# Dividing batch 0's outer products by head pairs, with one copy into the matmul bank

## The chip, the cores and the metric

The kernel runs on one core of a Trainium2 chip. The metric is device time in microseconds of one execution. Three executions of the kernel before took 101.63, 102.16 and 102.23 us; the median is 102.16.

## What is computed

Polynomial linear attention is followed by a two-layer network without a gate. The shapes are 4 batches, 4 heads, 1088 positions, head size 32, sketch size 8; 4352 tokens of 128 numbers, a hidden layer of 2048.

```python
a = einsum('rd,bhsd->bhsr', S1, x); b = einsum('rd,bhsd->bhsr', S2, x)
phi(x) = outer product of a and b, 64 features per position
kv = einsum('bhsf,bhsd->bhfd', phi(k), v);  z = phi(k).sum(over positions)
attn = (phi(q) @ kv) / (phi(q) @ z + 1e-6)
x = attn as (4352, 128)
h = x @ w_in;  g = h - tanh(h);  out = g @ w_out
```

## The kernel before

Every operation is an object with a name, the engines that may run it, and the tiles it reads and writes (`P.add`). A table of tokens (`TABLE`, line 27) sets the order: each token is the number of an operation, the letter of its engine (v VectorE, a ScalarE, g GpSimd, t TensorE, s SyncE) and, after a colon, the buffer or PSUM bank that a tile takes from its list. Every engine runs its own tokens strictly in the order of the table, and waits on semaphores for what it depends on (`sync`, line 244). `F` and `f` are fill matmuls on zeros at the start. Operations marked `lock` on VectorE and GpSimd wait for the other engine's last locked operation ahead of them in the table.

The work on keys, per batch b: transposes `kT` (line 579), the two sketches of the keys by matmul (`ksk`, line 599), their transposes back (`kab`, line 610), the Gram matrix of the two sketches (`gram`, `gm`, `scmm`, line 616 on), which gives the denominator; the outer products `w` of the two sketches, 64 per position and head (`k_outer`, and `k_outer0` for batch 0), and their product with v (`kvmm`, line 688). For queries: a transpose `qT`, sketches, a division and the outer products `qp`, their transposes `qpT`, and the numerators `num` (line 886), whose copies `x` (line 890) are the network's input `xT`.

Batch 0's first 384 columns take a way of their own, so that the network can start early (`q_lead`, line 743): the expanded sketches by matmul (`qA`, `qB`), the copies `bq0` and `bq1` of the second one out of PSUM on ScalarE, the products `qp0.0` and `qp0.1`, the denominator (`qac`, `abt`, `m0.0`, `den0.0`, `rd0.0`, `rdT`), the numerators `num0.0a` and `num0.1a`, and the tiles `x0.0a` and `x0.1a`. The remaining queries of batch 0 are transposed by `qT0.1` and run through `qsk0.3`, `abc0.3` and so on to `num0.3`.

Batch 0's keys: the tile `abk0` holds both sketches of all 9 blocks of 128 positions; its inner layout is (e, r, i), where head h = 2r + e, so `kab0.0` fills the head pair r = 0 and `kab0.1` the pair r = 1. `k_outer0` (line 670) cuts the nine blocks into four products, (0, 2), (2, 4), (4, 6) and (6, 9), all four heads in each. GpSimd makes the first two from SBUF (512 elements each), VectorE the other two (512 and 768 elements). For VectorE's two, ScalarE first copies the second sketch into a PSUM bank (`bps0`, `bps1`, line 678), and the product reads one operand from that bank (line 680). Each product has its own group of matmuls with v (`kvmm0.0` to `kvmm0.3`), which add up in the tile `pv[0]`. The result is copied and turned (`kvt0`, `kvt0t`, `kvc0`) for the numerators.

The network (`ffn`, line 972) takes ten groups of columns, 384, 352, 352, six times 512, and 192, with 16 blocks of the hidden layer each: `h` (line 984) into a PSUM bank, tanh `th` on ScalarE (line 988), from group 5 on for some columns the addition `dg` on VectorE (line 993), then `o` (line 1005), which adds up over the 16 blocks. The term without tanh goes through the combined weights `wch` and `wcl` (line 1009) where `dg` does not take it. The weights are cast to bf16 (`wi0` to `wi3`, `wo0` to `wo3`, line 934) and turned by the transposes `wit` (line 948) and their copies `wiT` (line 954). The output is transposed (`ot`, line 1014) and stored (`st`, line 1023).

PSUM has eight banks. Groups 0 to 6 use banks 0 to 2 for `h`, and bank 3 for the sum of `o`. The list `first1` (line 378), from which the small results of the head take a bank, leaves out bank 3.

Of the kernel before, what the change touches and what calls it, by code (L numbers as in the profile page):

```python
# [14 lines left out]
ALU = mybir.AluOpType  # L15
# [17 lines left out]
37s 237g 290t 31s 267t:2 268a:9 240a 269t:0 270a:10 132t:0 121v:1 41s 32s 273t:1 274a:11 279t:2 291t 35s 36s 292t 293t
280a:12 283t:0 284a:13 294t 271t:1 272a:14 122v:1 125v:1 275t:2 134v:0 43s 276a:15 89t:5 90a:0 133v 135t:3 136a:1
277t:0 278a:16 126v:0 123g:2 124v 44s 241g 246t:1 247t 137t 248a 57g 138v:0 139v 46s 285t:2 286a:17 295t 296t 55g
127t:0 53g 281t:0 129a 166v:1 165v 128v 297t 242g 298t 299t 13g 282a:18 48s 149v 316t:1 317a:19 322t:2 323a:0 318t:0
319a:1 167t:1 168v:1 324t:1 325a:2 54g 110s 328t:2 140g:4 300t 301t 169v 365t:0 366a:20 338t:1 184v 339a:21 141g:0
150t:0 320t:0 329a:22 383t:1 384a:23 109s 142g:3 40s 151v:1 249t:2 321a:28 250t 175g:1 251t 252t 9g 152v:0 153v:0 253v
369t:1 370a:29 393t:0 394a:3 170t:0 38s 143t:1 171a:0 144t 145t 310t:1 254v 326t:0 311a:4 327a:26 154v:0 302t 303t
146v:0 147s 314t:2 315a:27 172t 389t:1 173v:1 174v 304t 47s 390a:5 312t:0 313a:6 379t:2 380a:24 14g 185t:0 58g 305v:0  # L40
308s 342t:0 330t:1 371t:0 331a:25 177g:2 155g:0 158v:0 159v:1 372a:30 385t:2 386a:31 343t 344t 345t 346t 332t:1 333a:8
347t 348t 334t:0 349t 391t:2 350t 336t:1 351t 352t 186v:0 353t 335a:7 392a:9 337a:10 148s:1 340t:0 377t:2 156g:1 157v
354t 381t:1 115s 355t 356t 357t 358t 341a:32 359t 160g:2 378a:33 161v 114s 176v:4 387t:0 360v:1 382a:14 201v:1 373t:2
374a:11 367t:1 368a:34 162t:0 163v 187g:1 188v:1 388a:35 189v:1 164a 375t:2 376a:15 111s 395t:1 396a:16 397t:0 398t
399t 190g:1 193g:0 400t 401t 448t:0 449a:12 200v 436t:2 437a:18 112s 307s 446t:1 447a:13 45s 178t:2 179t 180t 219v
181v:1 194v:0 432t:0 433a:17 450t:2 451a:4 430t:1 431a:6 202t:0 182s 204v:0 203v 479t:0 480a:27 420t:2 195g:1 402t
403t 421a:19 434t:1 435a:1 183s:2 404t 405t 501t:0 502a:28 191g:2 211g:0 196v 205t:3 438t:2 439a:0 206v:1 210g:3 406t
407t 207t 422t:1 423a:2 116s 208v:0 209v 475t:0 476a:26 408t 489t:2 220t:0 192v 490a:22 428t:1 429a:25 424t:0 409t
410t 411t 412t 425a:8 413t 426t:2 497t:1 221v:1 306s 222v:0 487t:0 223v:0 224v:0 427a:7 488a:10 197t:0 481t:2 477t:0
414t 498a:21 199a 415v:2 482a:32 113s 440t:1 441a:20 213t:2 212g:1 214t 215t 198v 478a:34 216v:2 495t:2 225g:0 230g:0  # L50
309s 496a:29 545t:1 217s 231v:1 218s:3 608t:0 452t:0 453t 454t 455t 609a:30 610v 546a:11 620t:2 547v 228g:1 621a:15
622v 456t 457t 363s 505t:0 506a:33 458t 557t:1 459t 460t 361s 558a:24 559v 442t:2 229v 443a:14 461t 444t:0 445a:23
226g:2 462t 463t 503t:1 504a:31 554t:2 555a:35 227v 464t 465t 485t:0 486a:5 466t 493t:1 494a:9 556v 467t 468t 469t
470v:0 471s 483t:2 533t:0 534a:3 535v 572t:1 573a:16 574v 232t:0 234v 507t:0 484a:19 499t:0 500a:2 233v 542t:1 543a:8
# [251 lines left out]
def _vp(n):  # L306
    return {"vector": (n / 0.96 + 85.0, n / 0.96 + 215.0)}
# [6 lines left out]
def _a(n):  # L314
    return {"scalar": (n * 0.8333 + 62.0, n * 0.8333 + 203.0)}
# [6 lines left out]
def _gt(n):  # L322
    return {"gpsimd": (n * 1.76 + 120.0, n * 1.76 + 175.0)}
# [14 lines left out]
def bass_polysketch_attn__then__act_tanh_shrink_kernel(  # L338
# [316 lines left out]
    wvs = {}  # L655
# [8 lines left out]
            in1=abh(1)[:, :, None, :].to_broadcast([128, 12, 8, 8]),  # L664
            op=ALU.mult), r=[ab], w=[wv], name=f"w{b}.{p}", lock=True)

    bps = [_Val(first1) for _ in range(2)]
    K0 = [(0, 2), (2, 4), (4, 6), (6, 9)]

    def k_outer0():  # L670
        fs = lambda x, a, z: abk0[:, x, a:z].rearrange("p k (c i) -> p (k c) i", i=8)
        for p, (a, z) in enumerate(K0):
            wv = wvs[0, p] = _Val(w_p)
            nx = (z - a) * 4
            far = a >= 4
            if far:
                bp = bps[p - 2]
                P.add(_a(nx * 8), lambda e, n, a=a, z=z, bp=bp, nx=nx: e.copy(bp.ap[:, 0:nx * 8].rearrange("p (x i) -> p x i", i=8), fs(1, a, z)), r=ab0, w=[bp], name=f"bps{p - 2}")
            bsrc = lambda far=far, a=a, z=z, p=p, nx=nx: bps[p - 2].ap[:, 0:nx * 8].rearrange("p (x j) -> p x j", j=8) if far else fs(1, a, z)
            P.add(_vp(nx * 64) if far else _gt(nx * 64), lambda e, n, wv=wv, nx=nx, bsrc=bsrc, a=a, z=z: e.tensor_tensor(  # L680
                out=wv.ap[:, 0:nx * 64].rearrange("p (x i j) -> p x i j", i=8, j=8),
                in0=fs(0, a, z)[:, :, :, None].to_broadcast([128, nx, 8, 8]),
                in1=bsrc()[:, :, None, :].to_broadcast([128, nx, 8, 8]),
                op=ALU.mult), r=ab0 + ([bps[p - 2]] if far else []), w=[wv], name=f"w0.{p}", lock=not far)

    pv = [_Val(att1 if b else first1) for b in range(B)]

    def kv_mm(b):
        prev = None
        kc = K0 if b == 0 else [(0, 3), (3, 6), (6, 9)]  # L690

        def part(e, n, p):
            for blk in range(*kc[p]):
                for h in range(4):
                    x = (blk - kc[p][0]) * 4 + (h if b else h % 2 * 2 + h // 2)
                    i = e.matmul(pv[b].ap[h * 32:(h + 1) * 32, 0:64],  # L696
                                 vL[b][:, h, blk * 32:(blk + 1) * 32],
                                 wvs[b, p].ap[:, x * 64:(x + 1) * 64],
                                 start=(blk == 0), stop=(blk == 8), skip_group_check=True)
            return i  # L700
# [382 lines left out]
```

## Time and profile before

| what | value |
|---|---|
| median of 3 runs | 102.16 us |
| the profiled execution's own time | 101.74 us |
| its span, first to last instruction | 99.5 us |
| TensorE busy | 92.4 us |
| VectorE busy | 77.2 us |
| ScalarE busy | 78.4 us |
| GpSimd busy | 37.4 us |
| granted TensorE clock | 1.000 |

The profile records one execution. Each row of its timeline gives the start, the length, the engine (PE is TensorE, PEld its weight loads, DVE VectorE, ACT ScalarE, POOL GpSimd, SPq the DMA queue of SyncE), the line of the kernel, the operation, the tiles, shapes and the number of instructions, and in brackets how long the engine was idle before it and what ended that. Line 367 is a helper for copies, so rows with this line are told apart by their tiles. Lengths of records overlap a little within an engine. The tile names are those of memory: PSUM is always `psb`, batch 0's copies `bq` are written `th`, and the tanh tiles are written `th`, `wi_f` or `wo_f`, since they reuse this memory.

### The profile page before, as it was taken

What the parts mean: (1) busy time and instruction counts of PE and PEld (TensorE: products, weight loads), DVE (VectorE), ACT (ScalarE), POOL (GpSimd) and SP (SyncE); (2) the same over time, 40 slices, a digit from 0 to 9 for tenths busy, and PEclk for the clock granted to TensorE, in tenths of its full rate; (3) what the DMA queues carried; (4) which work ended last, traced back from release to release, by engine and by line L of the source; (5) the groups of instructions that cost most, each with busy time, mean ns of one, the idle gap of its engine ahead of it and who ended that gap; (6) DMA issues with size and microseconds to landing.
All of it is one profiled execution on the core that took longest, in us unless ns stands there. A gap on an engine that the chain in (4) does not pass through costs nothing.

```text
span 99.5 us, 3133 instructions
## 1 busy us (share of the span) xinstructions
PE 92.4 (93%) x1301; PEld 47.0 (47%) x1310; DVE 77.2 (78%) x144; ACT 78.4 (79%) x156; POOL 37.4 (38%) x57
## 2 busy tenths in 40 slices
PE   5987879999999999999999999999999999999980
PEld 2323543375366565635446444444444444444660
DVE  3097979999897999987857796757878899878630
ACT  4005149997886896989988998799999999998860
POOL 4046335288989473399979900000000000000000
PEclk9999999999999999999999999999999999999999
DMA  2996978799950468001700031510330553321627
GB/s 77 284 284 195 349 258 270 213 311 368 267 167 7 98 187 281 15 8 17 185 21 7 13 75 26 80 30 0 50 47 0 85 77 60 50 33 28 100 42 104
DMA packets 25541, 11.86 MB, mean 119 GB/s; under 512 B 19512, under 2 KB 23352, under 8 KB 25528
## 3 DMA queue, kind: packets, MB, share of 16 engines
q1 hardware_dynamic: 24440, 11.54, 44.5%
q10 hardware_dynamic: 1088, 0.13, 0.9%
q8 instruction: 10, 0.16, 0.7%
q14 instruction: 3, 0.02, 0.1%
HBM read 9.34 MB, written 2.33 MB: 117 GB/s over the span
## 4 chain that ended last, share of the span: by engine, by line
PE 79%; DVE 7%; ACT 4%; DMA 4%; issue 2%; POOL 0%; DVEq 0%
PE psb L984 31%; PE psb L1005 29%; PE psb L882 6%; DMA kL<-in_k_dram 4%; PE psb L599 3%; PE psb L1009 3%; PE psb L821 3%; ACT th L988 2%; DVE w L680 1%; PE psb L696 1%; DVE kT L579 1%; ACT wo_f L988 1%; DVE qp L768 1%; PE psb L962 1%; PE psb L761 1%
## 5 line engine op out<-in xcount | busy, mean ns | idle before, releaser
L988 ACT ACTIVATE th<-psb 128x512 bf16<-128x512 f32 (+3 forms) x83 | 45.1, 604 | 3.6 <-PE psb L984 2.8
L984 PE MATMUL psb<-xT,wi 128*128 128x512 bf16 (+3 forms) x154 | 42.5, 347 | 1.1 <-issue 0.3
L1005 PE MATMUL psb<-th,wo 128*128 128x512 bf16 (+3 forms) x94 | 25.9, 348 | 0.0
L984 PEld LDWEIGHTS psb<-xT,wi 128*128 128x128 bf16 x160 | 14.7, 98 | 19.3 <-ACT th L988 3.4
L993 DVE TENSOR_TENSOR th<-psb,th 128x320 bf16<-128x320 f32 (+2 forms) x28 | 14.9, 550 | 4.3 <-ACT th L988 4.0
L988 ACT ACTIVATE wi_f<-psb 128x512 bf16<-128x512 f32 (+3 forms) x28 | 16.7, 617 | 0.9 <-PE psb L984 0.8
L988 ACT ACTIVATE wo_f<-psb 128x512 bf16<-128x512 f32 (+3 forms) x25 | 14.2, 620 | 1.0 <-PE psb L984 0.6
L864 POOL TENSOR_TENSOR qp<-ap,abc 128x768 f32<-128x768 f32 x9 | 13.4, 1512 | 3.1 <-DVE qp L864 3.0
L1005 PEld LDWEIGHTS psb<-th,wo 128*128 128x128 bf16 x96 | 9.2, 98 | 8.2 <-DVE ot L1014 1.2
L661 POOL TENSOR_TENSOR w<-abk 128x768 f32<-128x768 f32 x8 | 11.9, 1512 | 0.9 <-DVE m L838 0.9
L869 DVE STREAM_TRANSPOSE qpT<-qp 128x768 f32<-128x768 f32 x11 | 10.5, 961 | 0.6 <-POOL qp L864 0.4
L1005 PE MATMUL psb<-wi_f,wo 128*128 128x512 bf16 (+2 forms) x34 | 10.2, 340 | 0.0
L1014 DVE STREAM_TRANSPOSE ot<-psb 128x512 f32<-128x512 f32 (+3 forms) x10 | 6.3, 631 | 4.0 <-PE psb L1005 4.0
L1005 PE MATMUL psb<-wo_f,wo 128*128 128x512 bf16 (+2 forms) x29 | 9.1, 352 | 0.1
L579 DVE STREAM_TRANSPOSE kT<-kL 128x512 f32<-128x512 f32 (+3 forms) x10 | 5.8, 602 | 2.8 <-DMA kL<-in_k_dram 2.8
L993 DVE TENSOR_TENSOR wi_f<-psb,wi_f 128x192 bf16<-128x192 f32 (+2 forms) x10 | 5.7, 565 | 1.6 <-ACT wi_f L988 1.4
L882 PE MATMUL psb<-qpT,kvb 32*32 32x288 f32 (+3 forms) x256 | 6.0, 379 | 0.0
L993 DVE TENSOR_TENSOR wo_f<-psb,wo_f 128x320 bf16<-128x320 f32 (+2 forms) x10 | 5.2, 547 | 0.8 <-ACT wo_f L988 0.5
L696 PE MATMUL psb<-w,vL 128*32 128x64 f32 x288 | 5.1, 221 | 0.6 <-issue 0.6
L442 PE MATMUL psb<-zz 128*128 128x512 bf16 x11 | 4.5, 596 | 1.1 <-DVE zz L440 1.1
L367 ACT COPY th<-psb 128x384 f32<-128x384 f32 x2 | 1.0, 480 | 5.6 <-PE psb L761 5.6
L826 DVE STREAM_TRANSPOSE abc<-psb 128x1152 f32<-128x1152 f32 (+1 forms) x4 | 5.0, 1262 | 0.3 <-PE psb L821 0.3
(100 smaller groups left out, 97.9 us busy)
## 6 DMA issues: line engine op xcount, KB each, us to landing
vL<-in_v_dram SPq DMA_DIRECT2D x16, 144.0 KB, 3.5
kL<-in_k_dram SPq DMA_DIRECT2D x6, 272.0 KB, 4.1
qL<-in_q_dram SPq DMA_DIRECT2D x6, 272.0 KB, 4.2
wi_f<-in_moe_w_in_dram SPq DMA_DIRECT2D x4, 256.0 KB, 4.7
wo_f<-in_moe_w_out_dram SPq DMA_DIRECT2D x4, 256.0 KB, 4.3
out_dram<-ot SPq DMA_DIRECT2D x15, 64.0 KB, 2.0
kL<-in_k_dram SPq DMA_DIRECT2D x1, 544.0 KB, 4.1
out_dram<-ot SPq DMA_DIRECT2D x8, 48.0 KB, 2.9
```

Of the source, the lines that this page charges most:

```text
L579: P.add(_v(nb * 32 * (r1 - r0)), lambda e, n, e_=e_, nb=nb, r0=r0, r1=r1: e.transpose(kTv[b][r0].ap.rearrange("p (j u t r) -> p r j u t", ...
L661: P.add({**_v(768), **_gt(768)}, lambda e, n: e.tensor_tensor(out=wv.ap.rearrange("p (x i j) -> p x i j", i=8, j=8), in0=abh(0)[:, :, :, N ...
L696: i = e.matmul(pv[b].ap[h * 32:(h + 1) * 32, 0:64], vL[b][:, h, blk * 32:(blk + 1) * 32], wvs[b, p].ap[:, x * 64:(x + 1) * 64], start=(blk ...
L826: P.add(_vp(sn * 4), lambda e, n: e.transpose(abc.ap.rearrange("p k h f -> p h k f")[:, :, 0:s1 - s0, :], psa4[:, :, 0:sn].rearrange("p h ...
L864: P.add({**_v(cn * 256), **_gt(cn * 256)}, lambda e, n, qp=qp, c0=c0, cn=cn: e.tensor_tensor(out=qp.ap[:, 0:cn * 256].rearrange("p (x i j) ...
L869: P.add(_v(cn * 256), lambda e, n, qp=qp, o0=o0, cn=cn: e.transpose(qt.ap[:, o0 * 256:(o0 + cn) * 256], qp.ap[:, 0:cn * 256]), r=[qp], w=[ ...
L882: i = e.matmul(psa4[h * 32:(h + 1) * 32, g, 0:kn * 32], (kvn[g * 32:(g + 1) * 32, h, x, :] if b else kvn[g * 32:(g + 1) * 32, h // 2, h % ...
L984: P.add(_mm(n_), lambda e, n, jb=jb, hv=hv: e.matmul(hv.ap[:, jb % m * 512:jb % m * 512 + n_], wi[jb // 4].ap[:, (jb % 4) * 128:(jb % 4 + ...
L988: act = P.add(_a(n_ * m), lambda e, n, hv=hv, th=th: e.activation(out=th.ap.rearrange("p (u x) -> p u x", u=m)[:, :, 0:n_], in_=hv.ap.rear ...
L993: P.add(_vp(gc * m), lambda e, n, hv=hv, th=th: e.tensor_tensor(out=th.ap.rearrange("p (u x) -> p u x", u=m)[:, :, 0:gc], in0=hv.ap.rearra ...
L1005: fn = lambda e, n, x=x, st=st, sp_=sp_: e.matmul(ov.ap[:, 0:n_], wo[x // 4].ap[:, x % 4, :], ths[x][0].ap[:, ths[x][1] * 512:ths[x][1] * ...
L1014: P.add(_vp(n_), lambda e, n: e.transpose(ot.ap[:, 0:n_], ov.ap[:, 0:n_]), r=[ov], w=[ot], name=f"ot{gi}")
```

## The change

`k_outer0` divides batch 0's products by head pairs and blocks. Product 0 is pair 1 of blocks 0 to 3, product 1 is pair 0 of the same blocks, both on GpSimd, 512 elements each; products 2 and 3 are pair 0 and pair 1 of blocks 4 to 8, both on VectorE, 640 elements each. A product of GpSimd depends on its own pair's `kab` alone. One ScalarE copy of 160 elements (`bps`) into one bank serves both of VectorE's products. The matmuls with v become two groups of 36: `kvmm0.0` takes products 0 and 2, `kvmm0.1` products 1 and 3, alternating between them. The list `first1` gains bank 3. The table is replaced as a whole, three operations shorter.

In the new table, within the head: `bps` is ScalarE's first copy, followed by `gm0`, `wacs` and `bq1`; `bq0` and the small copy `sc0` run on VectorE, between `qp0.1` and `abt`, and `qp0.0` runs behind `abt`; `qT0.1` runs behind `x0.0a` instead of ahead of `qp0.1`. The Gram result takes bank 3. TensorE's order is `ksk`, `qA`, `qB`, `gram0`, `scmm0`, `kvmm0.0`, `qac`, `kvmm0.1`, `kvt0t`, `num0.1a`, `num0.0a`, then the first `h`; `wit0` and `wit1`, which stood ahead of the first `h`, follow `o0.2` and `h0.4`. `wiT0` on ScalarE stands behind `th0.9` instead of ahead of the first tanh; `wi1` is cast on GpSimd. `h0.13` stands ahead of `num0.3` instead of behind it. Later, `wch` runs on ScalarE and `gm2` on VectorE, `w2.1` and `qp1.3` on GpSimd, `qp2.0`, `qp3.0` and `aq3.0` on VectorE. The order of `h`, `th` and `o`, their banks, and the order of the stores differ throughout.

```diff
-    first1 = one(0, 1, 2, 4, 5, 6, 7)
+    first1 = one(0, 1, 2, 3, 4, 5, 6, 7)
...
-    bps = [_Val(first1) for _ in range(2)]
-    K0 = [(0, 2), (2, 4), (4, 6), (6, 9)]
+    bps = _Val(first1)
+    K0 = [(1, 0, 4), (0, 0, 4), (0, 4, 9), (1, 4, 9)]
 
     def k_outer0():
-        fs = lambda x, a, z: abk0[:, x, a:z].rearrange("p k (c i) -> p (k c) i", i=8)
-        for p, (a, z) in enumerate(K0):
+        fs = lambda x, rh, a, z: abk0.rearrange("p x k (e r i) -> p x r (k e) i", e=2, r=2)[:, x, rh, a * 2:z * 2]
+        for p, (rh, a, z) in enumerate(K0):
             wv = wvs[0, p] = _Val(w_p)
-            nx = (z - a) * 4
+            nx = (z - a) * 2
             far = a >= 4
-            if far:
-                bp = bps[p - 2]
-                P.add(_a(nx * 8), lambda e, n, a=a, z=z, bp=bp, nx=nx: e.copy(bp.ap[:, 0:nx * 8].rearrange("p (x i) -> p x i", i=8), fs(1, a, z)), r=ab0, w=[bp], name=f"bps{p - 2}")
+            if p == 2:
+                P.add(_a(160), lambda e, n, a=a, z=z: e.copy(
+                    bps.ap[:, 0:160].rearrange("p (r x i) -> p r x i", r=2, i=8),
+                    abk0.rearrange("p x k (e r i) -> p x r (k e) i", e=2, r=2)[:, 1, :, a * 2:z * 2]), r=ab0, w=[bps], name="bps")
...
-                op=ALU.mult), r=ab0 + ([bps[p - 2]] if far else []), w=[wv], name=f"w0.{p}", lock=not far)
+                op=ALU.mult), r=[ab0[rh]] + ([bps] if far else []), w=[wv], name=f"w0.{p}", lock=not far)
...
+                prods = []
+                for p in (z, z + 2):
+                    rh, a, b_ = K0[p]
+                    prods.append([(p, rh * 2 + e_, blk, (blk - a) * 2 + e_) for blk in range(a, b_) for e_ in range(2)])
...
+            for z in range(2):
+                prev = P.add(_pe(540, 210.0), lambda e, n, z=z: part0(e, n, z), r=[wvs[0, z], wvs[0, z + 2]] + vvals[0], w=[pv[0]],
+                             chain=prev, mode="128x32", name=f"kvmm0.{z}")
```

More of the change, by code (lines that the diff above doesn't have):

```diff
@@ L33 @@
[L33 to L42, printed above, removed]
@@ L71 @@
+820t 821t 822t 823t 824t 825t 826t 827t 783s 786s 785a 828t 829v:1 833s 830a 832a 831s
 """
@@ L694, in part @@
                 for h in range(4):
-                    x = (blk - kc[p][0]) * 4 + (h if b else h % 2 * 2 + h // 2)
+                    x = (blk - kc[p][0]) * 4 + h
                     i = e.matmul(pv[b].ap[h * 32:(h + 1) * 32, 0:64],
```

97 lines of the change are left out of this document (60 added, 37 removed).

## The prediction

> **What bounds the kernel now.** I read the page first, for who is busy and who ends last.
>
> ```profile
> span 99.5 us, 3133 instructions
> PE 92.4 (93%) x1301; PEld 47.0 (47%) x1310; DVE 77.2 (78%) x144; ACT 78.4 (79%) x156; POOL 37.4 (38%) x57
> PE 79%; DVE 7%; ACT 4%; DMA 4%; issue 2%; POOL 0%; DVEq 0%
> ```
>
> The last row is the chain that ended last: TensorE carries four fifths of it. What is left for a change is the time in which TensorE waits. The busy times by stage say where that lies (columns: stretch, its length, then busy time and instructions of PE, PEld, DVE, ACT, POOL).
>
> ```profile
> 10.00:15.00 5.00, 3.79 (x126) 2.45 (x115) 4.33 (x11) 1.51 (x6) 1.70 (x5) 1.00 0.86 301
> 15.00:22.50 7.50, 7.50 (x133) 3.53 (x133) 7.17 (x14) 7.50 (x19) 4.10 (x8) 1.00 0.86 267
> 25.00:95.00 70.00, 69.07 (x875) 35.44 (x884) 57.55 (x102) 63.70 (x120) 25.46 (x24) 1.00 0.33 71
> 50.00:55.00 5.00, 4.68 (x146) 2.77 (x147) 3.45 (x7) 4.34 (x9) 4.49 (x4) 1.00 0.05 10
> ```
>
> From 25 us on TensorE idles 0.93 us in 70. The head is another thing: until 15 us VectorE works nearly without a break and TensorE waits for it. From 15 to 22.5 us ScalarE (7.50 of 7.50) and VectorE (7.17) are both full. So I follow VectorE's timeline through the head; a group starts where the one before has ended, so the difference of two starts is what an instruction costs in its queue.
>
> ```profile
> 7.53 0.85 DVE L610 STREAM_TRANSPOSE abk<-psb 128x288 f32<-128x288 f32 x2 [0.29 <-PE psb L599]
> 8.93 0.69 DVE L680 TENSOR_TENSOR w<-abk,psb 128x512 f32<-128x512 f32 x1 [0.55 <-ACT psb L678]
> 9.53 0.55 DVE L768 TENSOR_TENSOR qp<-psb,th 128x384 f32<-128x384 f32 x1
> 10.00 0.94 DVE L680 TENSOR_TENSOR w<-abk,psb 128x768 f32<-128x768 f32 x1
> 10.86 0.90 DVE L591 STREAM_TRANSPOSE qT<-qL 128x704 f32<-128x704 f32 x1
> 11.69 0.52 DVE L768 TENSOR_TENSOR qp<-psb,th 128x384 f32<-128x384 f32 x1
> 12.13 0.36 DVE L780 STREAM_TRANSPOSE ap<-psb 128x192 f32<-128x192 f32 x1
> 12.99 0.27 DVE L784 TENSOR_REDUCE den<-m 128x12 f32<-128x108 f32 x1 [0.50 <-POOL m L782]
> 13.55 0.58 DVE L787 STREAM_TRANSPOSE rdb<-rd 128x384 f32<-128x384 f32 x1
> 14.24 0.62 DVE L803 TENSOR_TENSOR xT<-psb,rdb 128x192 bf16<-128x192 f32 x2
> 14.78 1.36 DVE L579 STREAM_TRANSPOSE kT<-kL 128x512 f32<-128x512 f32 x2
> 23.88 0.55 DVE L367 CAST xT<-psb 128x384 bf16<-128x384 f32 x1
> 24.34 1.30 DVE L591 STREAM_TRANSPOSE qT<-qL 128x1088 f32<-128x1088 f32 x1
> ```
>
> The reader should see that the first hidden matmul needs the x tiles of 14.24, and that these stand behind everything VectorE did since 7.53. ScalarE and TensorE beside it:
>
> ```profile
> 8.67 0.22 ACT L678 COPY psb<-abk 128x64 f32<-128x64 f32 x1
> 9.19 0.26 ACT L678 COPY psb<-abk 128x96 f32<-128x96 f32 x1
> 14.71 1.01 ACT L367 COPY wiT<-psb 128x1024 bf16<-128x1024 bf16 x1 [0.94 <-PE psb L948]
> 15.62 2.80 ACT L988 ACTIVATE th<-psb 128x384 bf16<-128x384 f32 x7
> 21.12 0.37 ACT L367 COPY kvb<-psb 128x256 f32<-128x256 f32 x1
> 8.80 0.38 PE L627 MATMUL psb<-abk 128*32 128x32 f32 x18
> 9.96 0.25 PE L636 MATMUL psb<-gm,s2r 128*32 128x8 f32 x8
> 10.51 0.85 PE L756 MATMUL psb<-qT,wac 32*32 32x192 f32 x16 [0.30 <-ACT wac L367]
> 11.29 0.99 PE L696 MATMUL psb<-w,vL 128*32 128x64 f32 x56
> 13.27 0.85 PE L799 MATMUL psb<-qp,kvc 64*32 64x192 f32 x16 [0.33 <-ACT kvc L367]
> 14.05 0.62 PE L948 MATMUL psb<-identb,wi 128*128 128x128 bf16 x8
> 14.91 0.50 PE L984 MATMUL psb<-xT,wi 128*128 128x384 bf16 x2 [0.24 <-DVE xT L803]
> 19.55 0.33 PE L984 MATMUL psb<-xT,wi 128*128 128x384 bf16 x1
> 22.55 1.25 PE L882 MATMUL psb<-qpT,kvb 32*32 32x192 f32 x64
> ```
>
> **The change, part by part.** Times after the change are forecasts, worked out from differences of the starts above.
>
> The copy into the bank (bps) stands first on ScalarE, no longer behind bq0. The sketches are out at 8.38 (7.53 + 0.85), so it starts at about 8.45. Its 160 elements lie between 96 (0.26) and 256 (0.37): I take 0.31. VectorE's first product then starts near 8.80 instead of 8.93: 0.13 won.
>
> VectorE's two products have 640 elements each, where 512 cost 0.60 (8.93 to 9.53) and 768 cost 0.86 (10.00 to 10.86). Twice 0.73 is the same 1.46; both are done at 10.26. The new operands step over the other pair's elements. The nearest rows are these two on POOL: L661 reads blocks of eight that follow each other, L864 blocks that lie 32 apart, both in 1512 ns. So the stride costs 0; its bounds are 0 and, were it twice as slow, 1.46.
>
> ```profile
> L864 POOL TENSOR_TENSOR qp<-ap,abc 128x768 f32<-128x768 f32 x9 | 13.4, 1512 | 3.1 <-DVE qp L864 3.0
> L661 POOL TENSOR_TENSOR w<-abk 128x768 f32<-128x768 f32 x8 | 11.9, 1512 | 0.9 <-DVE m L838 0.9
> ```
>
> POOL's first product needs one sketch transpose instead of two and starts 0.4 earlier. That is hidden: the pair's matmuls wait for VectorE's half too.
>
> bq1 now stands behind gm0 and wacs. The Gram matmuls still end near 9.2; gm0, the matmuls of L636 (0.25, no longer behind kvmm0.0) and wacs, with some 0.1 for each hand-over, put bq1 at 9.93 to 10.41 and qp0.1 at 10.45: a new wait of 0.19. At 0.44 (11.69 to 12.13) it is through at 10.89.
>
> sc0 and bq0 move to VectorE, ahead of abt: 0.12 for eight columns (an estimate, below the 0.22 that the 64 columns of L678 take) and 0.46 for 384 (23.88 to 24.34). abt starts at 11.47. The matmuls qac that it needs run after kvmm0.0, now 36 of them: 36/56 of 0.99 is 0.64, from about 9.65, so qac ends by 11.2. Hidden.
>
> qT0.1 leaves its place ahead of qp0.1: 0.83 won (10.86 to 11.69). From abt on the order is as before but for qp0.0, which fits into the 0.50 wait for POOL. So everything is 12.13 − 11.47 = 0.66 earlier: x at 13.58, the first hidden matmul at 14.25. The other branch, kvmm0.1, kvt0, kvc0, the numerators, is no limit: the numerators start about 12.8 instead of 13.27.
>
> Against that, three things come back. The transposes wit0 and wit1 (14.05, in the gap ahead of the first hidden matmul) go into the busy run: with an overlap of 0.17 between their records and the next, 0.45 more TensorE work. wiT0 on ScalarE goes between the tanhs: 0.91 (14.71 to 15.62). But the first tanh, which had to wait for wiT0 until 15.62, comes as soon as its matmul is out (0.33 of L984 and a hand-over): about 14.62, so ScalarE stands 0.09 better at the same point. And qT0.1 is only moved: behind x it puts kT1 at 13.58 + 0.54 + 0.83 = 14.95, where it started at 14.78. VectorE runs in the same order from there to qpT0.3, with no idle time to take up, so num0.3 (22.55) starts at 22.72. This is why I do not carry the 0.66 to the end: num0.3 stands ahead of every group 1 matmul on TensorE's queue, since those need its x tiles.
>
> wi1 moves from ScalarE to POOL, into the 1.54 us that POOL idles ahead of wo0, whose load is only then there: 0, and at worst about the 0.61 of a cast of this size. The loads' order on SP is the same up to 25 us; later kvw1 stands behind one load more, the issue of one DMA, with the whole of batch 1's products ahead of its reader: 0.
>
> ```profile
> 15.07 0.61 POOL L367 CAST wo<-wo_f 128x512 bf16<-128x512 f32 x1 [1.54 <-DMA wo_f<-in_moe_w_out_dram]
> ```
>
> The bank added to the list holds the Gram result; fill matmuls and group 0's output use it long before and after: 0. The later order exchanges work between VectorE and POOL (w2.1, qp1.3 to POOL; qp2.0, qp3.0, aq3.0 back), neither of them full there (57.55 and 25.46 of 70): 0 as a sum, unknown as stalls.
>
> The sum at num0.3: 0.17 later, and the work behind it on TensorE is one hidden matmul less (h0.13 now stands ahead of num0.3): two records of 384 columns take 0.50 and one takes 0.33, so 0.17. The sum is zero. Behind it the lists hold the same matmuls. What the new order does with the 0.93 us of idle time there is the unknown: below, all of it goes (−0.93); above, every 5 us loses what the worst stretch lost (0.32, 50 to 55): 14 times that is 4.48, so +3.55. I take no change, the nearest row being the 70 us themselves. Span 99.5, own time 101.74; the median shown, 102.16, is 0.42 above that execution. **Forecast 102.2.**
>
> **The rivals.** (a) *The head's gain goes through.* If the VectorE chain is shorter than I count, TensorE's own list sets num0.3: 14.25, the 7.64 from 14.91 to 22.55, 0.45 for the transposes and 0.17 for h0.13 make 22.51, so 0.2 won with h0.13 counted. If half a microsecond of its waits for ScalarE in that stretch goes too, and half of the 0.93 behind it, that is 1.2: 101.0. Against it: VectorE's 7.17 of 7.50.
>
> (b) *The banks of the hidden layer come free too late.* From 55 us on a bank is held by ScalarE and then by VectorE's addition (L993), and the new order pairs other groups. If the idle time goes from 0.07 to 0.17 us per 5 us, that is 1.4: 103.5. It decides slower from 0.14 on, and the row of 50 to 55 shows that 0.32 can be. Against it: ScalarE's 63.70 of 70 leaves 6.3 us.
>
> (c) *The change does not do what it says*: if bq1's way over gm0 and wacs takes 0.66 more, x comes as before, and qT0.1 behind it puts off num0.3 by its whole 0.83; less 0.17 for h0.13 that is 0.66, so 102.8. Against it: the three small steps on that way sum to some 0.7 already, hand-overs counted.
>
> (d) *TensorE slows down.* Its fill matmuls began slowly:
>
> ```profile
> 1.12 4.53 PE L442 MATMUL psb<-zz 128*128 128x512 bf16 x11 [1.12 <-DVE zz L440]
> 48.23 0.60 PE L984 MATMUL psb<-xT,wi 128*128 128x512 bf16 x2
> 49.41 0.81 PE L984 MATMUL psb<-xT,wi 128*128 128x512 bf16 x3
> ```
>
> Eleven in 4.53 are 0.41 each; later one more costs 0.21 (0.81 − 0.60). With the transposes gone the gap ahead of the first hidden matmul has less work; were the slow pace to come back for 4 us there, that is some 1.9 lost: 104.1. Against it: numerators end near 13.6, the gap is 0.6. The Trainium skill, "TensorE: Matmul & The Clock Gate", Part 1, says the clock halves after an idle window of about 3.4 us; by that rule, 0.6 of idle does nothing, and the trace agrees as far as it goes (granted clock 1.00 in every stretch above, and 0.41 against 0.21 at the start). By the page alone (d) would be nil.
>
> **How the numbers follow.** My forecast 0.50, (a) 0.14, (b) 0.28, (c) 0.05, (d) 0.03. Within 1% is 101.1 to 103.2, about what a measurement of this kernel can tell from no change. The forecast (101.3 to 103.1 by itself) and (c) lie inside; a little of each falls out above, a quarter of (b) falls in. Faster 0.13, same 0.55, slower 0.32. The range takes in (a)'s upper part and (b): 101.1 to 103.9.
>
> **What would show it.** Right: first hidden matmul near 14.25, VectorE's first product near 8.80, bq0 and sc0 on VectorE between qp0.1 and abt, num0.3 within 0.3 of 22.7, about 1 us of TensorE idle from 25 to 95. Wrong: num0.3 before 22.3 (a), idle time over 1.9 from 25 to 95 (b), a first hidden matmul after 14.7 (c), hidden matmuls of 384 columns more than 0.2 apart from one another at 16 us (d).

## The result and the profile after

| | before | after |
|---|---|---|
| median of 21 runs each | 102.1 us | 102.28 us |
| ratio | | 1.0033, 95% interval 1.0017 to 1.0049 |
| span of the profiled execution | 99.5 us | 99.9 us |

The ratios of this document leave out executions more than 1.5% longer than the fastest of the same kernel (two of the kernel before here, 103.46 and 103.77 us); the medians hold all. The change makes the kernel some 0.3% slower, which is no difference of the size the prediction set out to tell (1%). Part of it lies outside what the profile shows: an execution's own time exceeds its span by 2.34 us in the median after, and by 2.19 in the executions of the kernel before that ran beside the experiments; no trace shows what fills that time. The page of the kernel after: span, busy times, the chain that ended last.

```profile
span 99.9 us, 3146 instructions
...
PE 93.5 (94%) x1310; PEld 47.6 (48%) x1310; DVE 78.0 (78%) x147; ACT 77.5 (78%) x152; POOL 37.2 (37%) x57
...
PE 86%; DMA 4%; ACT 3%; DVE 3%; issue 1%
```

TensorE's part of the chain went from 79% to 86%, VectorE's from 7% to 3%. These shares alone don't say that the change took VectorE off the path: `e8_split_only` below, in the order of before and with its time, has 89% and 5%. The busy times by stage of the kernel after (columns as in the prediction):

```profile
10.00:15.00 5.00, 3.80 (x114) 2.24 (x102) 4.54 (x12) 0.93 (x4) 2.36 (x7) 1.00 0.91 303
15.00:22.50 7.50, 7.24 (x139) 4.29 (x139) 7.29 (x14) 7.34 (x19) 4.49 (x8) 1.00 0.93 294
25.00:95.00 70.00, 69.87 (x881) 34.89 (x880) 57.63 (x104) 63.49 (x119) 24.11 (x23) 1.00 0.30 67
```

In the second row TensorE, full before (7.50), now misses 0.26. The timeline of the kernel after, by engine, at the places that the prediction followed:

```profile
8.32 0.30 ACT L677 COPY psb<-abk 128x160 f32<-128x160 f32 x1 [5.63 <-DVE abk L610]
...
14.77 1.64 ACT L1010 ACTIVATE th<-psb 128x384 bf16<-128x384 f32 x4 [1.84 <-PE psb L1006]
...
8.65 1.55 DVE L681 TENSOR_TENSOR w<-abk,psb 128x640 f32<-128x640 f32 x2 [0.36 <-ACT psb L677]
...
10.30 0.56 DVE L790 TENSOR_TENSOR qp<-psb,th 128x384 f32<-128x384 f32 x1
...
11.39 0.38 DVE L802 STREAM_TRANSPOSE ap<-psb 128x192 f32<-128x192 f32 x1
...
13.65 0.68 DVE L825 TENSOR_TENSOR xT<-psb,rdb 128x192 bf16<-128x192 f32 x2 [0.24 <-PE psb L821]
...
15.08 1.33 DVE L579 STREAM_TRANSPOSE kT<-kL 128x576 f32<-128x576 f32 x2
...
20.60 1.92 DVE L891 STREAM_TRANSPOSE qpT<-qp 128x768 f32<-128x768 f32 x2
...
97.09 0.38 DVE L1036 STREAM_TRANSPOSE ot<-psb 128x192 f32<-128x192 f32 x1 [1.52 <-PE psb L1027]
...
9.78 0.77 PE L703 MATMUL psb<-w,vL 128*32 128x64 f32 x36
...
11.25 0.77 PE L703 MATMUL psb<-w,vL 128*32 128x64 f32 x36
...
13.07 0.85 PE L821 MATMUL psb<-qp,kvc 64*32 64x192 f32 x16 [0.42 <-ACT kvc L367]
...
14.39 0.66 PE L1006 MATMUL psb<-xT,wi 128*128 128x384 bf16 x3 [0.47 <-DVE xT L825]
15.31 0.34 PE L1006 MATMUL psb<-xT,wi 128*128 128x384 bf16 x1 [0.26 <-ACT th L1010]
15.58 0.68 PE L843 MATMUL psb<-qT,wq 32*32 32x192 f32 x32
...
22.61 0.33 PE L1006 MATMUL psb<-xT,wi 128*128 128x384 bf16 x1
22.86 1.25 PE L904 MATMUL psb<-qpT,kvb 32*32 32x192 f32 x64
```

The reader should follow three numbers. The first hidden matmul starts at 14.39, 0.52 earlier than before (14.91). num0.3 starts at 22.86, 0.31 later (22.55). And the last output transpose starts at 97.09, where the kernel before has

```profile
96.74 0.38 DVE L1014 STREAM_TRANSPOSE ot<-psb 128x192 f32<-128x192 f32 x1 [1.52 <-PE psb L1005]
```

so 0.35 later. From num0.3 to there it is 74.19 before (96.74 − 22.55) and 74.23 after, and 74.18 to 74.31 in the kernels below but e11 (74.86) and e12 (74.48): whatever is decided by num0.3 is carried to the end, and the gain of 0.52 is lost, with 0.31 on top, in the eight microseconds between the first hidden matmul and num0.3. That stretch is 7.64 long before (14.91 to 22.55) and 8.47 after. It is the measure for the experiments below. The first hidden matmul moves by up to 0.13 between runs of kernels whose head is the same (14.26 to 14.39 below), so the length of the stretch says more than its end, and of the 0.31 and 0.35, read from one execution of each kernel, up to that much can be chance.

### The profile page after: what moved, and what is told of

Read it like the earlier page. It is cut to its first block, busy times and chain, and to the rows that moved or that the text cites. A ratio compares the mean times of both kernels' runs of the same rounds, so it can differ in the third digit from the quotient of the medians.

```text
span 99.9 us, 3146 instructions
## 1 busy us (share of the span) xinstructions
PE 93.5 (94%) x1310; PEld 47.6 (48%) x1310; DVE 78.0 (78%) x147; ACT 77.5 (78%) x152; POOL 37.2 (37%) x57
## 4 chain that ended last, share of the span: by engine, by line
PE 86%; DMA 4%; ACT 3%; DVE 3%; issue 1%
PE psb L1006 31%; PE psb L1027 30%; PE psb L904 6%; DMA kL<-in_k_dram 4%; PE psb L718 3%; PE psb L843 3%; PE psb L1031 3%; ACT th L1010 2%; PE psb L599 2%; PE psb L783 1%; PE psb L703 1%; DVE kT L579 1%; PE psb L627 1%; PE psb L984 1%; PE psb L970 1%
## 5 line engine op out<-in xcount | busy, mean ns | idle before, releaser
L1010 ACT ACTIVATE th<-psb 128x512 bf16<-128x512 f32 (+3 forms) x79 | 42.9, 593 | 5.1 <-PE psb L1006 5.0
L1015 DVE TENSOR_TENSOR th<-psb,th 128x192 bf16<-128x192 f32 (+2 forms) x27 | 13.8, 528 | 5.2 <-ACT th L1010 4.8
L1010 ACT ACTIVATE wo_f<-psb 128x512 bf16<-128x512 f32 (+3 forms) x29 | 16.4, 583 | 0.9 <-PE psb L1006 0.5
L661 POOL TENSOR_TENSOR w<-abk 128x768 f32<-128x768 f32 x9 | 13.5, 1516 | 1.8 <-DVE abk L610 1.8
L886 POOL TENSOR_TENSOR qp<-ap,abc 128x768 f32<-128x768 f32 x8 | 12.0, 1511 | 5.3 <-DVE qp L886 5.1
L1027 PE MATMUL psb<-wo_f,wo 128*128 128x512 bf16 (+2 forms) x34 | 10.4, 340 | 0.0
L579 DVE STREAM_TRANSPOSE kT<-kL 128x576 f32<-128x576 f32 (+3 forms) x10 | 5.8, 600 | 2.5 <-DMA kL<-in_k_dram 2.5
L1015 DVE TENSOR_TENSOR wi_f<-psb,wi_f 128x640 bf16<-128x640 f32 (+2 forms) x10 | 6.6, 660 | 1.1 <-ACT wi_f L1010 0.9
L591 DVE STREAM_TRANSPOSE qT<-qL 128x1088 f32<-128x1088 f32 (+2 forms) x5 | 5.3, 1063 | 0.0
L1027 PEld LDWEIGHTS psb<-wi_f,wo 128*128 128x128 bf16 x36 | 3.4, 98 | 2.8 <-DVE ot L1036 0.5
```

The lines of the kernel that those rows point to most:

```text
L579: P.add(_v(nb * 32 * (r1 - r0)), lambda e, n, e_=e_, nb=nb, r0=r0, r1=r1: e.transpose(kTv[b][r0].ap.rearrange("p (j u t r) -> p r j u t", ...
L591: P.add(_v((z - a) * 32), lambda e, n: e.transpose(tv.ap, qL[b][:, a * 32:z * 32]), r=vals, w=[tv] if b < 3 else [x[2] for x in qTv[0][1:] ...
L661: P.add({**_v(768), **_gt(768)}, lambda e, n: e.tensor_tensor(out=wv.ap.rearrange("p (x i j) -> p x i j", i=8, j=8), in0=abh(0)[:, :, :, N ...
L886: P.add({**_v(cn * 256), **_gt(cn * 256)}, lambda e, n, qp=qp, c0=c0, cn=cn: e.tensor_tensor(out=qp.ap[:, 0:cn * 256].rearrange("p (x i j) ...
L1010: act = P.add(_a(n_ * m), lambda e, n, hv=hv, th=th: e.activation(out=th.ap.rearrange("p (u x) -> p u x", u=m)[:, :, 0:n_], in_=hv.ap.rear ...
L1015: P.add(_vp(gc * m), lambda e, n, hv=hv, th=th: e.tensor_tensor(out=th.ap.rearrange("p (u x) -> p u x", u=m)[:, :, 0:gc], in0=hv.ap.rearra ...
```

## The experiments

Three theories were put to the test, and the expectations name them by letters. V: VectorE's chain to `qpT0.3` sets num0.3, as the prediction had it. T: TensorE's own list of matmuls sets it. S: ScalarE's unbroken run of tanhs, which frees the banks of `h`, sets it. Lines of the order are shown by the operations' names. Unless it is said otherwise, an experiment alters the kernel after; none leaves out a part of the computation.

### One engine given more work: e1, e2, e3

`e1_pe_plus` makes the eight transposes of `wit0` and `wit1`, four each, twice (the second result overwrites the first):

```diff
-                for j in range(z * 4, z * 4 + 4):
+                for j in list(range(z * 4, z * 4 + 4)) * (2 if i == 0 else 1):
```

> The changed kernel with the eight transposes wit0 and wit1 done twice each into the same place: 0.45 us more TensorE work ahead of num0.3, nothing else. The changed kernel stands at 1.0033 of before. Theory V (VectorE's chain sets num0.3, TensorE has cover ahead of it): num0.3 stays within 0.15 of 22.86 and the ratio at 1.003. Theory T (TensorE's own list sets num0.3): num0.3 at about 23.3, ratio 1.0077. Theory S (ScalarE's run of tanhs sets it): ratio 1.003.

`e2_dve_plus` adds a reduction of 640 columns on VectorE behind `qT0.1`, into a tile that nobody reads at that time:

```diff
+    P.add(_v(640), lambda e, n: e.tensor_reduce(
+        out=rdb.ap[:, 0:20], in_=kL[1][:, 0:640].rearrange("p (a b) -> p a b", b=32), op=ALU.add, axis=AX.X),
+        r=kvals[1], w=[rdb], name="extra")
```

> The changed kernel with a reduction of 640 columns, used by nobody, behind qT0.1 on VectorE: some 0.75 us more VectorE work behind the x tiles and ahead of num0.3. Theory V: num0.3 at about 23.6, ratio 1.0107. Theory T: VectorE has what lies between its last transpose and num0.3 to give, about 0.2, or more if something is hidden earlier: num0.3 later by 0.4 at most, ratio up to 1.007. Theory S: as T.

`e3_act_plus` casts `wo1` on ScalarE twice, first into an unused tile:

```diff
-copy(e, n, wo[i].ap[:, :, :], wof[i].ap)
+[copy(e, n, o_[:, :, :], wof[i].ap) for o_ in ([junk] if i == 1 else []) + [wo[i].ap]][-1]
```

> The changed kernel with the cast wo1 done twice on ScalarE, the first time into a tile that nobody reads: 0.5 us more ScalarE work between the seventh and the eighth tanh. Theory S: later by about 0.5, ratio 1.008. Theories V and T: ScalarE's tanhs are needed by TensorE some matmuls later, ratio 1.003 to 1.005.

Measured: e1 102.65 us, ratio 1.0078 (1.0053 to 1.0103); e2 102.73, 1.0086 (1.0065 to 1.0107); e3 103.11, 1.0116 (1.0093 to 1.014). TensorE's timeline of e1, e2 and e3, one fence each:

```profile
14.39 0.66 PE L1006 MATMUL psb<-xT,wi 128*128 128x384 bf16 x3 [0.47 <-DVE xT L825]
...
23.30 1.25 PE L904 MATMUL psb<-qpT,kvb 32*32 32x192 f32 x64
```

```profile
14.26 0.66 PE L1006 MATMUL psb<-xT,wi 128*128 128x384 bf16 x3 [0.47 <-DVE xT L825]
...
21.24 0.38 PE L627 MATMUL psb<-abk 128*32 128x32 f32 x18 [0.47 <-DVE abk L610]
...
23.27 1.25 PE L904 MATMUL psb<-qpT,kvb 32*32 32x192 f32 x64
```

```profile
14.39 0.66 PE L1007 MATMUL psb<-xT,wi 128*128 128x384 bf16 x3 [0.47 <-DVE xT L826]
...
19.28 0.82 PE L1028 MATMUL psb<-th,wo 128*128 128x384 bf16 x4 [0.26 <-ACT th L1011]
...
23.31 1.25 PE L905 MATMUL psb<-qpT,kvb 32*32 32x192 f32 x64
```

The stretch grows from 8.47 to 8.91, 9.01 and 8.92. All of the 0.45 that e1 gives to TensorE arrives (0.44), which V and S rule out and T asks for; `qpT0.3` stays at 20.60 there, so VectorE's chain is through 0.78 ahead of num0.3. But most of what e2 and e3 give arrives as well (0.54 of the reduction's 0.69, 14.95 to 15.64; 0.45 of the cast's 0.51, 17.69 to 18.20), and the rows show how: not at num0.3 but at an earlier matmul of TensorE's list, which now waits 0.47 for VectorE's sketches of batch 1 (e2) or 0.26 for a tanh (e3). So TensorE's list sets num0.3 in the kernel after, and the two other engines run so close behind it that work of half a microsecond on either comes through. No theory with one engine alone holds. e3's median is longer than the stretch explains (1.0116, where e1 with the same stretch has 1.0078; the intervals overlap); whether there is more behind it stays open.

### The weight transposes back ahead of the first hidden matmul: e4

The order of `e4_wit_back`: `wit0`, `wit1`, `wiT0` and the two small steps on GpSimd that they need in order go back, and the banks of `h` change places accordingly:

```diff
+ wit0 (TensorE), wit1 (TensorE), first h:bank 0, wiT0 (ScalarE), first tanh, h:bank 1, h:bank 2, ...
- first h:bank 0, first tanh, h:bank 2, h:bank 1, ... wit0, ... wit1, ... wiT0
```

> The changed kernel with one part undone: wit0 and wit1 stand ahead of the first hidden matmul again and wiT0 ahead of the first tanh; the banks of the first hidden matmuls are picked so that none waits for another's. 0.45 us of TensorE work and 0.9 us of ScalarE work leave the run. The first tanh is put off from 14.8 to about 15.1. Theory V: num0.3 stays near 22.7, the ratio between 1.002 and 1.0035. Theory T: num0.3 comes up to VectorE's limit, 22.7, and the ratio to 1.0017. Theory S: as T. If TensorE then waits ahead of num0.3 for VectorE, that is V with the numbers of both.

Measured: 102.84, 1.0094 (1.0074 to 1.0115); none of the theories had it slower than the kernel after. TensorE's and VectorE's timeline of e4:

```profile
14.41 0.50 PE L1006 MATMUL psb<-xT,wi 128*128 128x384 bf16 x2
15.59 0.73 PE L1006 MATMUL psb<-xT,wi 128*128 128x384 bf16 x2 [0.69 <-ACT wiT L367]
...
17.05 0.98 DVE L848 STREAM_TRANSPOSE abc<-psb 128x768 f32<-128x768 f32 x1 [0.62 <-PE psb L843]
```

The transposes are free there (the first `h` at 14.41), but ScalarE's copy behind them is not: the third hidden matmul takes bank 2, where the transposes lie until they are copied, and waits 0.69; the queries' sketches stand behind that matmul in TensorE's queue, and VectorE waits 0.62 for the sketches (17.05 against 16.38). num0.3 is at 23.46. The kernel before has the same copy in the same place and its first tanh no earlier, at 15.62, but its queue has only two hidden matmuls ahead of the sketches, and so none that has to wait; the sketches start at 15.34. So e4 put a wait of its own into TensorE's list and does not decide between the theories.

### VectorE relieved, or held up ahead of x: e5, e6, e7

`e5_qT_back` puts `qT0.1` back ahead of `qp0.1`. `e6_relax_dve` gives `sc0` and `bq0` back to ScalarE and puts `qT0.1` between `qp0.1` and `abt`; `e7_combo` is e6 with e4's order.

```diff
- w0.3 qp0.1 ... sc0 (VectorE) ... bq0 (VectorE) abt ... x0.0a qT0.1        (after)
+ w0.3 qT0.1 qp0.1 ... sc0 (VectorE) ... bq0 (VectorE) abt ... x0.0a       (e5)
+ w0.3 qp0.1 ... sc0 (ScalarE) bq0 (ScalarE) qT0.1 ... abt ... x0.0a       (e6)
```

> The changed kernel with one part undone: qT0.1 stands ahead of qp0.1 on VectorE again. The x tiles come about 0.7 later (14.3), the first hidden matmul near 15.0, kT1 at 14.9 instead of 15.08. Theory V (VectorE's chain sets num0.3): the head's gain was worth nothing, num0.3 at 22.7, ratio 1.002 to 1.004. Theory T (TensorE's own list sets it): num0.3 at 23.3 to 23.6, ratio 1.008 to 1.010.

> The changed kernel with sc0 and bq0 on ScalarE behind bq1, where it is idle, and qT0.1 between qp0.1 and abt on VectorE. VectorE loses 0.6 of work and takes qT0.1 into its wait for qac: kT1 starts near 14.5 instead of 15.08, the x tiles stay within 0.2 of 13.65. Theory V: num0.3 comes 0.3 to 0.5 earlier, ratio 0.999 to 1.000. Theory T: nothing moves, ratio 1.003.

> The changed kernel with both relaxations: sc0 and bq0 on ScalarE, qT0.1 between qp0.1 and abt, and wit0, wit1 and wiT0 back ahead of the first hidden matmul. Theory V and theory T alike: both limits move by 0.4 to 0.6, num0.3 near 22.4, ratio about 0.999. If one bound alone mattered, one of the two single changes would have the same time as this; if both lie side by side, this gains more than either.

Measured: e5 102.52, 1.0054 (1.0029 to 1.0079); e6 102.35, 1.0027 (1.0002 to 1.0052); e7 102.81, 1.007 (1.0045 to 1.0095). The timeline of e6:

```profile
14.32 0.66 PE L1005 MATMUL psb<-xT,wi 128*128 128x384 bf16 x3 [0.47 <-DVE xT L824]
15.24 0.34 PE L1005 MATMUL psb<-xT,wi 128*128 128x384 bf16 x1 [0.26 <-ACT th L1009]
...
22.74 1.25 PE L903 MATMUL psb<-qpT,kvb 32*32 32x192 f32 x64
...
16.30 0.98 DVE L847 STREAM_TRANSPOSE abc<-psb 128x768 f32<-128x768 f32 x1 [0.76 <-PE psb L842]
```

In e6 VectorE has 0.76 to spare ahead of `abc0.3`, and nothing comes of it: the stretch is 8.42, within 0.05 of the kernel after. In e5 the first `h` is only 0.32 later (14.71), though 0.83 of work went ahead of it, since `qp0.1` had waited for `bq1` and x for the numerators anyway; the stretch is 8.41. Its num0.3 (23.12) and its ratio lie between what V and T had said; T's figures had the first hidden matmul at 15.0. What both runs show is that VectorE's work ahead of `abc0.3` doesn't set num0.3, since `abc0.3` has to wait for TensorE's sketches: the list takes 8.4 from the first hidden matmul on, whatever the slack there. VectorE's chain behind `abc0.3` is as long as in the kernel after in both; that it isn't the limit either is what e1 shows. e7 runs into the same wait for `wiT0` as e4 (0.68).

### The division of the products alone: e8

`e8_split_only` has the new products and the one copy, but everything else in the order of before; `kvmm0.0` stands behind the small matmuls of the Gram result, since its new form needs a product of VectorE.

```diff
-    first1 = one(0, 1, 2, 3, 4, 5, 6, 7)
+    first1 = one(0, 1, 2, 4, 5, 6, 7)
```

> The kernel before with one part of the change alone: the division by head pairs and the one copy, in the order of before (the first group of matmuls with v behind scmm0, two bank copies merged into the first one's place). Expected from the rows: the copy is 0.09 longer and still behind bq0, the two products cost the same 1.46 together. Both theories: within 0.2 us of before, ratio 0.998 to 1.002. If the products themselves were what costs the 0.3 per cent, the ratio would be 1.003.

Measured: 101.89, 0.9992 (0.9964 to 1.002). Its page, stages and timeline:

```profile
PE 93.9 (94%) x1310; PEld 47.2 (47%) x1310; DVE 77.2 (78%) x144; ACT 78.3 (79%) x155; POOL 37.3 (37%) x57
```

```profile
25.00:95.00 70.00, 69.97 (x885) 35.48 (x884) 57.61 (x102) 63.75 (x121) 24.68 (x23) 1.00 0.32 69
50.00:55.00 5.00, 5.00 (x148) 2.83 (x148) 3.45 (x7) 4.34 (x9) 4.55 (x4) 1.00 0.03 5
```

```profile
14.93 0.50 PE L1005 MATMUL psb<-xT,wi 128*128 128x384 bf16 x2 [0.36 <-DVE xT L824]
...
22.50 1.25 PE L903 MATMUL psb<-qpT,kvb 32*32 32x192 f32 x64
```

The stretch is 7.57 and the time that of before: the strided products cost nothing, and the longer stretch comes from the order (or from bank 3 in `first1`, which e8 leaves out too). The intervals of the two ratios, this one's and that of the kernel after, just overlap. The first two fences correct a reading of the prediction, below.

### The sketches moved ahead of the wait, and wo1 on GpSimd: e9 to e12

In the kernel after the fourth hidden matmul waits 0.26 for the first tanh, with the queries' sketches `qsk0.3` behind it, which could use that time. `e9_qsk_early` (on e6) puts them right behind the numerators `num0.0a`, which take bank 3 instead of 7; `e12_qsk_before_h4` (on e6) puts them between the third and the fourth hidden matmul. `e10_wo1_pool` is the kernel after with the cast of `wo1` on GpSimd instead of ScalarE, 0.51 less in the run of tanhs; `e11_qsk_wo1` is e9 with that cast.

```diff
- num0.0a:bank 7, h, h, h, h, qsk0.3, ... wo1 (ScalarE)                    (after)
+ num0.0a:bank 3, qsk0.3, h, h, h, h, ...                                  (e9)
+ wo0 (GpSimd), wi2 (GpSimd), wo1 (GpSimd)                                 (e10)
+ num0.0a:bank 7, h, h, h, qsk0.3, h, ...                                  (e12)
```

> As e6_relax_dve, and the query sketch qsk0.3 stands on TensorE right behind num0.0a, in the gap ahead of the first hidden matmul, instead of behind four hidden matmuls, the last of which waits for the first tanh; the casts it needs and the bank of num0.0a are moved for it. 0.54 us of TensorE work leave the run, and VectorE's abc0.3 no longer waits for it, so VectorE's chain is free to come 0.5 to 0.7 earlier. The first tanh starts about 0.15 later. Theories V and T: num0.3 at 22.2 to 22.4, ratio 0.998 to 0.999. Theory S (ScalarE's run of tanhs and copies sets it): num0.3 within 0.2 of 22.75, ratio 1.002 to 1.004.

> The changed kernel with the cast wo1 on GpSimd, in its idle time between wi2 and wi3, instead of on ScalarE between the seventh and eighth tanh: 0.5 us of ScalarE work leave the run, nothing else moves but wi3, by 0.6 at most. Theory S: the mirror of e3_act_plus, num0.3 at about 22.4, ratio 0.997 to 0.999. Theories V and T: num0.3 stays within 0.15 of 22.86, ratio 1.003. If e3_act_plus was a one-sided thing (another bound close behind), the gain is a part of 0.5.

> e9_qsk_early and e10_wo1_pool together: VectorE, TensorE and ScalarE all have about 0.5 us less ahead of num0.3. If the three bounds lie side by side there, as e1, e2 and e3 say when read together, only this one gains the whole: num0.3 at 22.2 to 22.3, ratio 0.997, that is faster than both kernels by some 0.3 to 0.6 us. If one bound alone counts, one of the two single changes has the same time.

> As e6_relax_dve, but the query sketches qsk0.3 stand ahead of the fourth hidden matmul, not behind it. In e6 TensorE waits 0.26 at that matmul for the first tanh (15.24), with qsk0.3 (0.54 from its start to the next) queued behind it. qsk0.3 uses no bank of the hidden layer and its input is there since 14.2. T (TensorE's own list sets num0.3): the wait is filled, qsk0.3 starts near 14.97, num0.3 at 22.74 - 0.26 = 22.48, ratio 1.000 (e6 had 1.0027). S (ScalarE's run of tanhs, full from 14.70, sets it): num0.3 stays within 0.05 of 22.74, ratio 1.003, and waits for a tanh show up later in TensorE's list. V (VectorE's chain sets it): abc0.3 comes some 0.5 earlier than e6's 16.30, and num0.3 would follow by as much. A fourth way, from e9: qsk0.3 breaks off in mid-sequence without any engine to wait for, the fourth hidden matmul comes later than 15.5, num0.3 after 22.9, ratio 1.005 or more.

Measured: e9 103.11, 1.0076 (1.0039 to 1.0114); e10 102.05, 1.0004 (0.9978 to 1.003); e11 105.16, 1.0171 (1.0106 to 1.0235); e12 102.32, 1.0046 (1.0018 to 1.0075). e11's ratio rests on two executions alone (103.2 and 104.3). The timelines of e9, e12 and e11, in this order:

```profile
13.66 0.57 PE L842 MATMUL psb<-qT,wq 32*32 32x192 f32 x22
14.84 0.54 PE L842 MATMUL psb<-qT,wq 32*32 32x192 f32 x10 [0.60 <-issue]
```

```profile
14.86 1.10 PE L842 MATMUL psb<-qT,wq 32*32 32x192 f32 x32
15.89 0.66 PE L1005 MATMUL psb<-xT,wi 128*128 128x384 bf16 x3
16.81 0.34 PE L1005 MATMUL psb<-xT,wi 128*128 128x384 bf16 x1 [0.26 <-ACT th L1009]
...
23.16 1.25 PE L903 MATMUL psb<-qpT,kvb 32*32 32x192 f32 x64
```

```profile
13.84 0.57 PE L842 MATMUL psb<-qT,wq 32*32 32x192 f32 x22
16.22 0.62 PE L842 MATMUL psb<-qT,wq 32*32 32x192 f32 x10 [1.80 <-issue]
```

In all three the sketches, which take 0.54 where they stand behind the fourth hidden matmul (15.51 to the next matmul at 16.05 in e6), break off and go on later: after 22 of 32 matmuls in e9 and e11, for 0.60 and 1.80, and in e12 their record is 1.10 long, with a break after 18. The profile names no engine and no transfer that TensorE waits for ("issue"), and the same instructions run through when they come at 15.34 (the kernel before) or later. In e12 the break eats the 0.26 that was to be won and more: the next hidden matmul starts at 15.89, so its tanhs are late, and the wait for a tanh comes back at 16.81. It is the fourth way of its expectation. Whether the sketches behind two hidden matmuls, as in the kernel before, would win back the 0.26 was not tried.

e10 is level with before by its interval, which overlaps that of the kernel after, so a gain over the kernel after is not shown. Inside the span there is none: the stretch is 8.71 (14.26 to 22.97), 0.24 longer than in the kernel after, and the median span of its twelve executions is 100.2 (99.9 after). Its lower median comes from outside the span, where it has 1.87 instead of 2.34; why, no trace shows. Its num0.3 is where V and T had it, not at S's 22.4. A row of its VectorE shows why the relief is worth nothing in the stretch:

```profile
17.59 0.36 DVE L859 TENSOR_TENSOR m<-abc 128x192 f32<-128x192 f32 x1 [0.36 <-POOL wo L366]
```

`wo1`'s cast is a locked operation, so VectorE's product `m0.3`, locked too, has to wait 0.36 for it, and the Gram matmuls of batch 1 then wait 0.27 for VectorE: ScalarE's relief is paid for by VectorE. No version tried beats the kernel before.

## Why the prediction was right, and where its reasons failed

The forecast was 102.2 and the median is 102.28; no change beyond 1% is right. The steps, one by one.

- **The head.** The copy at 8.32 (forecast 8.45), VectorE's first product at 8.65 (8.80), qp0.1 at 10.30 (10.45), abt at 11.39 (11.47): right, all some 0.1 early, as is the sketches' transpose ahead of them (7.44 against 7.53). The two products cost 1.47 from start to the next start (8.64 to 10.11 in e5), 1.46 in the forecast; the division costs nothing.
- **"The other branch is no limit."** This step failed, by a little. VectorE could have started x at 13.41 (13.65 − 0.24), but it waited for the numerators, which started at 13.07 and not 12.8. The prediction gives no working for its 12.8. By its own terms the way is 9.65, 0.64 for `kvmm0.0`, 0.78 for `qac` (10.51 to 11.29 before), 0.64 for `kvmm0.1` and 0.99 from there to the numerators (12.28 to 13.27 before): 12.70. Measured are 9.78, 0.69, 0.78, 0.77 and 1.05, together 13.07: the mis-sized term is mainly the matmuls with v, whose 36 take more than 36/56 of the 56. The first hidden matmul is at 14.39 instead of 14.25.
- **VectorE's chain to num0.3: 0.17 later.** `qpT0.3` went from 20.43 to 20.60, the 0.17 of the forecast. That it is so exact is luck: `kT1` was 0.30 later (15.08), and 0.13 of this came back by the product `m0.3` (17.39 against 17.22).
- **"num0.3 waits for that chain."** This is the step that failed. The transposes are through at 22.52 (20.60 + 1.92), and TensorE was busy with its list until num0.3 at 22.86. In the kernel before it is the same: the row quoted in the prediction has TensorE at 7.50 of 7.50 from 15 to 22.5, which leaves no room for a wait at 22.55. I looked at VectorE's 7.17 and passed over the fuller number beside it. (ScalarE has 7.50 there too; e1 to e3 tell the engines apart in the kernel after alone.) TensorE's list adds up: 0.52 earlier, 0.45 for the transposes (e1: 0.44), 0.17 for `h0.13`, 0.26 for the wait for the first tanh, together 0.36 later, measured 0.31. Rival (a) had this list, without that wait and with a first `h` at 14.25, and so it came out early.
- **"0.17 less behind num0.3."** It did not show: from num0.3 to the last output transpose it is 74.23 after and 74.19 before. Both orders keep TensorE full there (69.97 of 70 in e8, 69.87 after), so the new one gives about 0.2 back; where, the traces do not settle.
- **"TensorE idles 0.93 us in 70", and 0.32 in the worst five.** This reading was wrong, and rivals (a) and (b) and both bounds were built on it; so was the sign "about 1 us of TensorE idle", where the kernel after shows 0.13. The page of before has 1301 matmuls and 1310 weight loads: nine records are missing, and their places look like idle time. e8, with the same later order, has all 1310, and there the 70 us hold 0.03 of idle time and the stretch from 50 to 55 none. Of the other kernels those with nine records short show 68.7 to 68.9 in these 70 us (e11, at a lowered clock, 68.3), the complete ones 69.8 to 70.0, and yet both kinds take the same 74.2 from num0.3 to the last transpose (e1, e2 and e4, short of nine, 74.22 to 74.23; e5, e6 and the kernel after, complete, 74.23 to 74.24): the idle time is not there.
- **Rival (d), the slow clock**, did not happen in the kernel after (granted clock 1.00 in the stretches shown); it happened in e11, below.

So the time was forecast nearly right because the whole exchange is small beside what a measurement tells, not because every step held; this is luck in part. The two terms that were mis-sized go the same way: num0.3 0.14 later than forecast, and 0.21 less won behind it, together the 0.35 by which the end of the span moved. The largest single error, the engine that sets num0.3, cost little here because VectorE's chain and TensorE's list end within 0.34 of one another. What is shown: the head's half microsecond is spent inside TensorE's own list, most of it on work that the change itself moved there. In the kernel before, `wit0` and `wit1` fill a gap in which TensorE waits anyway.

## What to carry to other kernels

Ask for each stage which engine's queue has no gap at all ahead of the point that counts; an engine at 96% next to one at 100% is the second limit, not the first. Work that sits in a gap is free there: an order that makes the gap shorter and moves the work into the full stretch has gained only the difference. Before idle time of TensorE is counted as room, compare the number of matmul records with that of the weight loads.

## What the runs showed of the hardware

The clock dropped after a short pause. In e11 TensorE stood still from 14.4 to 16.2, and soon after the granted clock fell to one half for more than three microseconds (busy times of e11 by microsecond, the granted clock third from the end):

```profile
15.00:16.00 1.00, 0.00 (x0) 0.00 (x0) 0.60 (x2) 0.00 (x0) 0.00 (x0) 1.00 0.90 312
16.00:17.00 1.00, 0.78 (x11) 0.29 (x12) 0.11 (x1) 0.00 (x0) 0.65 (x1) 0.77 0.92 303
17.00:18.00 1.00, 1.00 (x4) 0.26 (x2) 0.87 (x1) 0.69 (x2) 0.32 (x1) 0.50 0.79 228
18.00:19.00 1.00, 1.00 (x3) 0.21 (x2) 0.57 (x2) 1.00 (x4) 0.52 (x3) 0.50 0.92 307
19.00:20.00 1.00, 1.00 (x5) 0.49 (x5) 0.88 (x4) 0.79 (x3) 0.46 (x1) 0.52 1.06 367
20.00:21.00 1.00, 1.00 (x13) 0.74 (x11) 0.91 (x1) 0.55 (x3) 0.01 (x1) 1.00 1.01 343
```

The pause is the 1.80 of the broken-off sketches. The Trainium skill, "TensorE: Matmul & The Clock Gate", Part 1, puts the idle window at about 3.4 us; here a pause of about half that was followed by the drop, and full speed is back some 3.4 us after the drop (0.46 of the first of these microseconds at half clock, two whole ones, 0.96 of the next), which agrees with the page's figure for the busy window. Whether the sparse matmuls ahead of the pause counted as idle cannot be told from this run. The mean granted clock was 0.967 to 0.984 in five of e11's six executions and in three of e9's seven, and 0.983 in one of the 31 of the kernel before that ran beside e5 to e8; e9's profiled execution, with its pause of 0.60, kept the full clock until 99.9 us.

The break in `qsk0.3` was not expected either. It needs no engine and no bank. In all three kernels it comes at the same place of TensorE's list, behind its 220th matmul (e9, e11) or 219th (e12), though in e12 three hidden matmuls more stand ahead of the sketches; so it hangs on the place in the list and not on the sketches. The traces also hold DMA packets of a kind called instruction. The first of these with 16 KB starts at 12.50 in e9, 13.76 in e11 and 13.10 in e12, and TensorE goes on 2.34, 2.46 and 2.31 later (14.84, 16.22, 15.41). In the eleven kernels without the break, before and after among them, the 221st matmul comes 2.65 to 4.08 after that packet's start. So that TensorE's next instructions were not yet there fits all fourteen traces; it was not tried by itself, by moving that packet.
